# Attention and two expert layers in one kernel: the third tile of scores, the loads of q and k, and the shared tile

## The chip, the core and the metric

The kernel runs on one core of a Trainium2 chip. The time is device microseconds of one execution. The engines are TensorE (PE; its weight loads are listed apart as PEld), VectorE (DVE), ScalarE (ACT), GpSimd (POOL) and SyncE (SP), which here only issues DMAs. A letter q behind an engine's name means its sequencer, which issues DMAs.

## The reference

Three stages follow each other: causal attention of 2 batches x 12 heads, 448 positions, width 64; a layer 768 -> 2048 -> 768 with a leaky activation (slope alpha for each of the 2048); a second one with a piecewise quadratic activation. The 24 heads make 12 pairs.

```
scores = q @ k.T / sqrt(64), masked above the diagonal
attn   = softmax(scores);  x = attn @ v          # 896 tokens x 768
h = x @ w_in;   x = (max(h,0) + alpha*min(h,0)) @ w_out
h = x @ w2_in;  x = where(h>=1, h, where(h<=-1, 0, (h+1)**2/4)) @ w2_out
```

The weights arrive as 64-bit floats and are converted on the chip.

## The kernel before, in words

**Attention** handles one pair of heads at a time. The 448 queries of a head are three tiles of 128 and a rest of 64. Tiles 0, 1, 2 see 128, 256 and 384 keys. The two rests of a pair share one 128-row tile (the shared tile, NQ in the code), whose 448 scores come from one product: the stationary operand `qdiag` (128x128) holds the rest of one head in its upper left quarter and that of the other in its lower right one, with zeros elsewhere.

The loop at the end of the program runs over periods p = 0 to 13, and in period p three pairs are worked on: the scores of pair p (`scores`, L357 on, matmuls L376 and for the shared tile L372), their masking and row minimum on DVE (L383), exponentials on ACT (`expo`, L392), the scaling by the row sums on POOL (`norm`, L399 to L403, with a reciprocal on DVE, L400); for pair p-1 the transposes on PE (`transp`, L430) with copies out of PSUM on ACT and DVE (L439); for pair p-2 the product with v (`attnv`, L446 and L454) and the split of its result x into two parts (`evac_x`, L213 on ACT, L216 on DVE). Every engine works in the order in which the program is written. On PE a period is: scores of tiles 0 and 1, the shared tile, attnv of p-2, transposes of tiles 0 and 1 of p-1, scores of tile 2, transposes of the shared tile and of tile 2 of p-1.

**Banks.** PSUM has 8 banks: s0, s1 (scores, one for each head; tiles 0 and 1 share them, tile 2 takes them again), s2 (shared tile), o (attnv), and two each of t0 and t1 (transposes, L410). A group of matmuls on a bank waits until the readers of its last use are done; for s0 and s1 these are the DVE instructions of L383.

**Loads.** `load` (L330 to L340) brings q and k of one pair (448 KB, L336) and the two quarters of `qdiag` (16 KB each, L340); three buffers each. `load_v` (L342 to L348) brings v in seven pieces. Weights (`Weights.load`, L103) come in chunks of 768 or 512 KB into two buffers. All of them are issued by SP, one after the other, in the order of the program. `prime` converts the first chunks during attention: the magnitude on ACT (L113), then from period 4 on one of five steps per period (four on DVE at L129, L135, L141, L153; the fourth one is L147 on DVE with a cast on ACT, L150).

**The layers** (`run_layer`, matmuls L253) follow with 2304 matmuls of 128x448; a few of them (`early_tiles`) fill the last periods of attention.

Of the kernel before, what the change touches and what calls it, by code (L numbers as in the profile page):

```python
# [8 lines left out]
F32 = mybir.dt.float32  # L9
# [13 lines left out]
def attention_moe_moe_kernel(ctx: ExitStack, tc: tile.TileContext, qk, v, w1, w2, w3, w4, alpha, out):  # L23
# [8 lines left out]
    nc = tc.nc  # L32
    NP, _, _, S = qk.shape
    NB = 2
    CP, D = v.shape[1], v.shape[-1]
# [30 lines left out]
    def warm_up():  # L66

        z = const.tile([128, 512], F32R, tag="zero", name="zero")
        nc.vector.memset(f32(z), 0.0)
        for _ in range(NWARM):  # L70
            ps = ps_o.tile([128, 512], F32, tag="o", name="warm_ps")
            nc.tensor.matmul(ps, lhsT=z[:, :128], rhs=z, start=True, stop=True)

    def constants():
        nc.vector.memset(half, 0.5)
        make_identity(nc, ident)
        for t, p0, n in ((mask, 0, Q), (mask_rest, 0, D), (mask_rest, D, D)):
            if p0 == 0:
                nc.gpsimd.memset(t, 0.0)
            d = t[p0:p0 + n, t.shape[1] - n:]  # L80
            nc.gpsimd.affine_select(
                out=d, in_=d, compare_op=ALU.is_ge, fill=MASK, base=0, pattern=[[-1, n]], channel_multiplier=1
            )


    class Weights:
# [82 lines left out]
        def next(self):  # L169
            self.n_used += 1  # L170
            return self.split.pop(self.n_used - 1)
# [66 lines left out]
    def new_banks():  # L238

        pools = (ps_s, "s0"), (ps_s, "s1"), (ps_s, "s2"), (ps_o, "o"), (ps_t, "t0"), (ps_t, "t1"), (ps_t, "t0"), (ps_t, "t1")  # L240
        while True:
            for pool, tag in pools:
                yield pool.tile([128, 512], F32, tag=tag, name="ps")
# [17 lines left out]
    def early_tiles(batches):  # L261

        for f, bs in enumerate(batches):
            ws = wts.next()
            ps = {b: new_tile() for b in bs}
            early[f] = ws, ps
            for k in range(KD - 1):
                products(ps, ws, x_t, k, k, k == 0, False)
                yield

    def run_layer(layer, late):

        if layer in (1, 3):
            mt, nch, kc, src = NF, 1, KD, x_t
        else:
            mt, nch, kc, src = NM, NC2, KC, g_t
        evac = {1: act_prelu, 2: evac_x, 3: act_quad, 4: evac_out}[layer]
        for m in range(mt):
            ps = {}
            for ch in range(nch):  # L280
                if layer == 1 and m in early:
                    ws, ps = early.pop(m)
                    products(ps, ws, src, kc - 1, kc - 1, False, True)
                else:
                    ws = wts.next()
                rest = {b: new_tile() for b in range(NB) if b not in ps} if ch == 0 else ps

                end = layer == 4 and m == mt - 1 and ch == nch - 1
                for group in [{b: p} for b, p in rest.items()] if end else [rest] if rest else []:
                    for k in range(kc):  # L290
                        kk = ch * kc + k
                        products(group, ws, src, k, kk, kk == 0, kk == nch * kc - 1)
                    if end:
                        interleave(*(evac(p, m, b) for b, p in group.items()), [])
                ps = {**ps, **rest}
                if wts.n_used > 1 and not early:
                    interleave(wts.split_ops(), late)
                    late = []
                    wts.load()
                    wts.magnitude()  # L300
            late = [] if end else [op for pair in zip(*(evac(ps[b], m, b) for b in range(NB))) for op in pair]
        return late


    class Attention:
# [51 lines left out]
        def scores(self, p, tiles):  # L357
            if 0 in tiles:
                self.pexp[p] = self.ap.tile([Q, 2, TRI], F32, tag="pexp", name="pexp", bufs=3)
                self.st[p] = self.ap.tile([Q, 2, 2 * NQ + 1], F32, tag="stat", name="stat", bufs=4)  # L360
            t = self.raw[p]
            if NQ in tiles:
                banks = [self.ps_s.tile([128, 512], F32, tag="s2", name="rest_ps")]
            else:
                banks = [self.ps_s.tile([128, 512], F32, tag=f"s{j}", name=f"s{j}_ps") for j in range(2)]
            off, todo = 0, []
            for i in tiles:
                for n, (e, col) in enumerate(self.rows(p, i)):
                    w = e.shape[1]
                    ps = banks[n][:, off:off + w]  # L370
                    if i == NQ:
                        nc.tensor.matmul(ps, lhsT=self.qdiag[p % 3], rhs=t[:, 1, :], start=True, stop=True)  # L372
                        todo.append((e, ps, mask_rest, col))
                    else:
                        h = slice(n * D, (n + 1) * D)
                        nc.tensor.matmul(  # L376
                            ps, lhsT=t[h, 0, i * Q:(i + 1) * Q], rhs=t[h, 1, :w], start=True, stop=True
                        )
                        todo.append((e, ps, mask[:, REST - w:], col))
                off += w  # L380

            for e, ps, m, col in todo:
                nc.vector.tensor_tensor_reduce(  # L383
                    out=e, in0=ps, in1=m, scale=-SCALE, scalar=3.0e38, op0=ALU.add, op1=ALU.min,
                    accum_out=self.st[p][:, 0, col:col + 1],
                )
# [76 lines left out]
    with tc.manual_schedule():  # L463
        wts = Weights()
        ps_s, ps_t, ps_o = (
            ctx.enter_context(tc.tile_pool(name=f"ps_{n}", bufs=b, space=PSUM))
            for n, b in (("s", 1), ("t", 2), ("o", 1))
        )
        banks = new_banks()
        with ExitStack() as pa:  # L470
            ap = pa.enter_context(tc.tile_pool(name="attn", bufs=2))
            at = Attention(ap, ps_s, ps_t, ps_o)
            at.zeros()
            at.load(0)
            warm_up()
            at.load(1)
            at.load_v(0)
            nc.sync.dma_start(out=alpha_sb, in_=alpha)
            constants()
            early = {}  # L480
            fill = early_tiles(((0, 1), (0,)))
            prime = wts.prime()
            PRIME = 3

            for p in range(NP + 2):
                new, mid, old = p < NP, 1 <= p <= NP, p >= 2  # L490

                def spare():
                    if not new:
                        next(prime, None)
                        next(fill, None)

                if new:
                    at.scores(p, (0, 1))
                    at.scores(p, (NQ,))
                    at.expo(p, (0, 1, NQ))  # L500
                spare()
                if old:
                    at.attnv(p - 2)
                    high, low = at.evac(p - 2)
                    high()
                if p >= PRIME:
                    next(prime, None)
                if mid:
                    at.transp(p - 1, (0, 1))
                if new:  # L510
                    at.scores(p, (2,))
                if old:
                    low()
                if new:
                    at.expo(p, (2,))
                spare()
                if mid:
                    at.transp(p - 1, (NQ,))
                    at.transp(p - 1, (2,))
                if new:  # L520
                    at.norm(p)
                spare()
                if 0 < p < NP - 1:
                    at.load(p + 1)
                if p + 1 < NP:
                    at.load_v(p + 1)
                if p == PRIME - 2:
                    wts.load()
                    wts.load()
            for _ in fill:  # L530
                pass
            for _ in prime:
                pass
        gpool = ctx.enter_context(tc.tile_pool(name="g", bufs=1))
        ep = ctx.enter_context(tc.tile_pool(name="ep", bufs=2))
        late = []
        for layer in (1, 2, 3, 4):
            late = run_layer(layer, late)
            if layer % 2 == 0:
                interleave(late, [])  # L540
                late = []
# [44 lines left out]
```

## Time and profile before

| | |
|---|---|
| median of 3 runs (range) | 563.89 us (562.46 to 571.53) |
| the profiled execution | 563.78 us |
| its span, first to last instruction | 561.9 us |
| PE, PEld busy | 97%, 86% |
| DVE, ACT, POOL busy | 74%, 43%, 24% |
| matmuls of the layers (L253), busy | 234.7 + 233.8 us |
| granted TensorE clock, mean | 0.993 |

The profile is one execution; its span is 1.9 us shorter than its time. The share of a busy engine is a mean over the attention (the first 96 us), where all engines work in turns, and the layers, where PE works nearly alone. Times in the rows are microseconds from the start of the span; idle time in brackets stands before the instruction, with what ended it.

### The profile page before, as it was taken

How to read it: one execution, taken by the hardware profiler on the slowest of the kernel's cores; microseconds unless marked ns; L12 is line 12 of the kernel's file. 1: busy time of each engine (PE TensorE's matmuls, PEld its weight loads, DVE VectorE, ACT ScalarE, POOL GpSimd, SP SyncE). 2: the span in 40 equal slices, each digit the busy share in tenths (PEclk: the TensorE clock that was granted, in tenths of full speed). 3: DMA queues.
4: the chain of work that ended last, by engine and by line, in shares of the span. 5: the costliest groups of instructions: out<-in, count | busy, mean ns of one | idle time of the engine just before them, and what ended most of it. 6: DMA issues, size and time to landing. Idle time of an engine off the chain costs nothing.

```text
span 561.9 us, 8739 instructions
## 1 busy us (share of the span) xinstructions
PE 547.4 (97%) x3195; PEld 482.2 (86%) x3195; DVE 418.4 (74%) x797; ACT 240.6 (43%) x509; POOL 136.6 (24%) x179
## 2 busy tenths in 40 slices
PE   7699999999999999999999999999999999999997
PEld 3456667999999999999999999999999999999996
DVE  4569886888888998765765779888888867555740
ACT  5578984333333333322233345555555433222220
POOL 4526753133333331000000003333333300000000
PEclk9889999999999999999999999999999999999999
DMA  4544511333333223433333523333322244343421
GB/s 122 199 136 117 167 55 58 112 113 113 113 113 113 75 76 113 127 98 113 114 112 88 177 97 108 113 113 113 113 95 75 76 129 143 132 130 128 145 71 33
DMA packets 25674, 62.31 MB, mean 111 GB/s; under 512 B 5280, under 2 KB 13984, under 8 KB 25632
## 3 DMA queue, kind: packets, MB, share of 16 engines
q1 hardware_dynamic: 23760, 60.15, 34.5%
q10 hardware_dynamic: 1872, 1.61, 0.8%
q8 instruction: 25, 0.41, 0.3%
q14 instruction: 17, 0.14, 0.1%
HBM read 58.99 MB, written 2.75 MB: 110 GB/s over the span
## 4 chain that ended last, share of the span: by engine, by line
PE 84%; POOL 0%; DVE 0%; ACT 0%; issue 0%; ACTq 0%
PE ps L253 83%; PE o_ps L446 0%; PE t_ps L430 0%; POOL pexp L403 0%; PE o_ps L454 0%; DVE o_sb L226 0%; ACT o_sb L226 0%; ACTq L226 0%
## 5 line engine op out<-in xcount | busy, mean ns | idle before, releaser
L253 PE MATMUL ps<-x,w_split 128*128 128x448 f32 x1152 | 234.7, 366 | 0.0
L253 PE MATMUL ps<-g,w_split 128*128 128x448 f32 x1152 | 233.8, 365 | 0.0
L253 PEld LDWEIGHTS ps<-g,w_split 128*128 128x128 f32 x1152 | 216.3, 188 | 17.1
L253 PEld LDWEIGHTS ps<-x,w_split 128*128 128x128 f32 x1152 | 216.0, 188 | 17.4
L177 POOL TENSOR_TENSOR g<-act_g,g 128x448 fp32r<-128x448 f32 x64 | 85.5, 1336 | 271.3 <-ACT g L176 271.2
L150 ACT CAST w_split<-w_f 128x512 fp32r<-128x512 f32 (+1 forms) x80 | 56.6, 707 | 125.8 <-DVE w_f L147 86.7
L153 DVE TENSOR_TENSOR w_split<-w_f,w_split 128x512 fp32r<-128x512 f32 (+1 forms) x80 | 66.1, 827 | 52.6 <-ACT w_split L150 52.5
L176 ACT CAST g<-act_g 128x448 fp32r<-128x448 f32 x64 | 36.2, 565 | 76.8 <-DVE act_g L189 62.8
L129 DVE TENSOR_SCALAR w_f<-w_f 128x512 f32<-128x512 f32 (+1 forms) x80 | 58.5, 731 | 9.0 <-ACT w_f L113 8.9
L147 DVE SCALAR_TENSOR_TENSOR w_f<-w_raw,w_f 128x512 uint32<-128x512 uint32 (+1 forms) x80 | 63.6, 795 | 1.4
L141 DVE SCALAR_TENSOR_TENSOR w_f<-w_raw,w_f 128x512 uint32<-128x512 uint32 (+1 forms) x80 | 63.5, 794 | 1.4
L113 ACT ACTIVATE w_f<-w_raw 128x512 f32<-128x512 f32 (+1 forms) x80 | 61.2, 764 | 0.4 <-DMA w_raw<-w 0.4
L392 ACT ACTIVATE pexp<-pexp,stat 128x128 f32<-128x128 f32 (+2 forms) x72 | 35.8, 499 | 16.8 <-DVE stat L383 16.5
L135 DVE TENSOR_SCALAR w_f<-w_f 128x512 uint32<-128x512 uint32 (+1 forms) x80 | 38.2, 478 | 1.4
L201 ACT ACTIVATE act_t<-act_t,half 128x448 f32<-128x448 f32 x32 | 21.5, 672 | 37.7 <-DVE act_t L200 37.7
L403 POOL TENSOR_SCALAR pexp<-pexp,stat 128x128 f32<-128x128 f32 (+2 forms) x72 | 34.5, 494 | 4.7 <-DVE stat L383 3.3
L383 DVE CUSTOM_DVE_ANT_0 pexp<-s_ps,mask 128x128 f32<-128x128 f32 (+2 forms) x72 | 26.2, 413 | 9.6 <-PE s_ps L376 9.2
L376 PE MATMUL s_ps<-qk_raw 64*128 64x128 f32 (+2 forms) x144 | 25.4, 431 | 5.6 <-DMA qk_raw<-qk 4.8
L226 DVE COPY o_sb<-ps 128x224 f32<-128x224 f32 x12 | 4.7, 391 | 29.8 <-ACT o_sb L226 29.8
L439 DVE COPY pt<-t_ps 128x128 f32<-128x128 f32 (+2 forms) x36 | 14.0, 418 | 13.1 <-PE t_ps L430 13.1
L446 PEld LDWEIGHTS o_ps<-pt,v 128*64 128x64 f32 x144 | 9.7, 143 | 14.9 <-ACT pt L439 6.0
L200 DVE TENSOR_SCALAR act_t<-ps 128x448 f32<-128x448 f32 x32 | 19.9, 622 | 3.0 <-PE ps L253 2.4
(47 smaller groups left out, 280.4 us busy)
## 6 DMA issues: line engine op xcount, KB each, us to landing
w_raw<-w SPq DMA_DIRECT2D x32, 768.0 KB, 4.3
w_raw<-w SPq DMA_DIRECT2D x48, 512.0 KB, 3.7
qk_raw<-qk SPq DMA_DIRECT2D x11, 448.0 KB, 3.9
out<-o_sb SPq DMA_DIRECT2D x12, 112.0 KB, 1.7
out<-o_sb ACTq DMA_DIRECT2D x12, 112.0 KB, 1.7
v<-v SPq DMA_DIRECT2D x12, 56.0 KB, 2.7
v<-v SPq DMA_DIRECT2D x12, 48.0 KB, 2.1
v<-v SPq DMA_DIRECT2D x12, 40.0 KB, 2.0
```

Of the source, the lines that this page charges most:

```text
L113: nc.scalar.activation(out=f32(w), in_=f32(hi), func=AF.Abs)
L129: nc.vector.tensor_scalar(out=f32(w), in0=f32(w), scalar1=HI_MIN, scalar2=HI_MAX, op0=ALU.max, op1=ALU.min)
L135: nc.vector.tensor_scalar(out=w, in0=w, scalar1=5, scalar2=2, op0=ALU.logical_shift_left, op1=ALU.logical_shift_right)
L141: nc.vector.scalar_tensor_tensor(out=w, in0=hi, scalar=0xC0000000, in1=w, op0=ALU.bitwise_and, op1=ALU.bitwise_or)
L147: nc.vector.scalar_tensor_tensor(out=w, in0=lo, scalar=29, in1=w, op0=ALU.logical_shift_right, op1=ALU.bitwise_or)
L150: nc.scalar.copy(s[:, 0, :n], f32(w))
L153: nc.vector.tensor_sub(s[:, 1, :n], f32(w), f32(s[:, 0, :n]))
L176: nc.scalar.copy(t[:, 0, :], g)
L177: nc.gpsimd.tensor_sub(t[:, 1, :], g, f32(t[:, 0, :]))
L253: nc.tensor.matmul(ps[b][:, :S], lhsT=ws[:, part, k * 128:(k + 1) * 128], rhs=src[b, kk][:, xp, :], start=first and part == 0 and xp == 0, ...
L392: nc.scalar.activation(out=e, in_=e, func=AF.Exp, bias=st[:, 0, col:col + 1], scale=-1.0, accum_out=st[:, 1, col:col + 1],)
L403: nc.gpsimd.tensor_scalar(out=e, in0=e, scalar1=sums[:, col:col + 1], scalar2=1.0, op0=ALU.mult, op1=ALU.mult)
```

## The change

It has four parts. The third tile of scores of pair 0 goes into the banks t0 and t1 instead of s0 and s1. In period 1 the third tile of scores stands ahead of the transposes of pair 0. The load of q and k of pair p+2 is issued in period p (before: of pair p+1, and none in period 0), and the first two chunks of weights are issued in periods 1 and 2, one in each, behind that load (before: both in period 1). The product of the shared tile is two matmuls, each with 64 columns of `qdiag` and 64 partitions of the result.

```diff
--- before.py
+++ after.py
@@ -362,14 +362,21 @@
             if NQ in tiles:
                 banks = [self.ps_s.tile([128, 512], F32, tag="s2", name="rest_ps")]
             else:
-                banks = [self.ps_s.tile([128, 512], F32, tag=f"s{j}", name=f"s{j}_ps") for j in range(2)]
+
+                pool, tag = (self.ps_t, "t") if p == 0 and 2 in tiles else (self.ps_s, "s")
+                banks = [pool.tile([128, 512], F32, tag=f"{tag}{j}", name=f"{tag}{j}_ps") for j in range(2)]
             off, todo = 0, []
             for i in tiles:
                 for n, (e, col) in enumerate(self.rows(p, i)):
                     w = e.shape[1]
                     ps = banks[n][:, off:off + w]
                     if i == NQ:
-                        nc.tensor.matmul(ps, lhsT=self.qdiag[p % 3], rhs=t[:, 1, :], start=True, stop=True)
+
+                        for j in range(2):
+                            h = slice(j * D, (j + 1) * D)
+                            nc.tensor.matmul(
+                                ps[h], lhsT=self.qdiag[p % 3][:, h], rhs=t[:, 1, :], start=True, stop=True
+                            )
                         todo.append((e, ps, mask_rest, col))
                     else:
                         h = slice(n * D, (n + 1) * D)
@@ -505,9 +512,11 @@
                     high()
                 if p >= PRIME:
                     next(prime, None)
+                if p == 1:
+                    at.scores(p, (2,))
                 if mid:
                     at.transp(p - 1, (0, 1))
-                if new:
+                if new and p != 1:
                     at.scores(p, (2,))
                 if old:
                     low()
@@ -520,12 +529,11 @@
                 if new:
                     at.norm(p)
                 spare()
-                if 0 < p < NP - 1:
-                    at.load(p + 1)
+                if p + 2 < NP:
+                    at.load(p + 2)
                 if p + 1 < NP:
                     at.load_v(p + 1)
-                if p == PRIME - 2:
-                    wts.load()
+                if p in (PRIME - 2, PRIME - 1):
                     wts.load()
             for _ in fill:
                 pass
```

The order of PE's matmuls, from the shared tile of period 0 to the end of period 1, before (s_ps and rest_ps are scores, t_ps is a bank of t0 or t1):

```order
L372 MATMUL rest_ps<-qk_raw,qdiag_83 128x448
L376 MATMUL s_ps<-qk_raw 128x384 x2
L376 MATMUL s_ps<-qk_raw 128x128 x2
L376 MATMUL s_ps<-qk_raw 128x256 x2
L372 MATMUL rest_ps<-qk_raw,qdiag_84 128x448
L430 MATMUL t_ps<-ident,pexp 128x64 x12
L376 MATMUL s_ps<-qk_raw 128x384 x2
L430 MATMUL t_ps<-ident,prest_91 128x64 x8
L430 MATMUL t_ps<-ident,pexp 128x64 x12
```

And the same stretch with the change (L377 and L383 are the matmuls of the scores there, L437 the transposes):

```order
L377 MATMUL rest_ps<-qk_raw,qdiag_83 64x448 x2
L383 MATMUL t_ps<-qk_raw 128x384 x2
L383 MATMUL s_ps<-qk_raw 128x128 x2
L383 MATMUL s_ps<-qk_raw 128x256 x2
L377 MATMUL rest_ps<-qk_raw,qdiag_84 64x448 x2
L383 MATMUL s_ps<-qk_raw 128x384 x2
L437 MATMUL t_ps<-ident,pexp 128x64 x12
L437 MATMUL t_ps<-ident,prest_91 128x64 x8
L437 MATMUL t_ps<-ident,pexp 128x64 x12
```

The 128x384 scores of pair 0 now write a t bank, those of pair 1 stand ahead of twelve transposes, and each shared tile is two products.

SP's DMAs behind the load of alpha, before (v_87, v_88 and v_89 are v of pairs 1, 2 and 3; the first qk_raw here is q and k of pair 2, the second of pair 3; six more pieces of v follow each first one):

```order
L478 DMA alpha_sb<-alpha 128x16
L348 DMA v_87<-v 112x128
...
L336 DMA qk_raw<-qk 128x896
L340 DMA qdiag_85<-qk 64x64 x2
L348 DMA v_88<-v 112x128
...
L103 DMA w_raw<-w 128x1536 x2
L336 DMA qk_raw<-qk 128x896
L340 DMA qdiag_83<-qk 64x64 x2
L348 DMA v_89<-v 112x128
```

With the change (the three qk_raw are pairs 2, 3 and 4):

```order
L485 DMA alpha_sb<-alpha 128x16
L336 DMA qk_raw<-qk 128x896
L340 DMA qdiag_85<-qk 64x64 x2
L348 DMA v_87<-v 112x128
...
L336 DMA qk_raw<-qk 128x896
L340 DMA qdiag_83<-qk 64x64 x2
L348 DMA v_88<-v 112x128
...
L103 DMA w_raw<-w 128x1536
L336 DMA qk_raw<-qk 128x896
L340 DMA qdiag_84<-qk 64x64 x2
```

Each load of q and k has moved ahead of the seven pieces of v that stood before it, and that of pair 3 ahead of both chunks of weights as well.

## Rows read from the trace of the kernel before

**Rows 1.** Chain of waits, its last long piece: start, duration, what.

```profile
96.13 462.29 PE ps L253 x2280
```

**Rows 2.** Busy time by stretch: stretch, length, engines (count), PE clock, DMA share, GB/s.

```profile
21.36:26.11 4.75, 0.00 (x1) 0.03 (x1) 1.82 (x6) 1.88 (x6) 3.08 (x8) 0.90 0.68 251
26.11:35.09 8.98, 8.53 (x75) 4.91 (x76) 3.61 (x17) 4.94 (x16) 0.53 (x1) 0.67 0.46 130
```

**Rows 3.** Timeline of PE, periods 2 to 10: start, duration, instruction, [idle before].

```profile
16.51 1.02 PE L372 MATMUL rest_ps<-qk_raw,qdiag 128*128 128x448 f32 x2
...
26.11 1.65 PE L376 MATMUL s_ps<-qk_raw 64*128 64x128 f32 x8 [4.75 <-DMA qk_raw<-qk]
27.69 1.86 PE L372 MATMUL rest_ps<-qk_raw,qdiag 128*128 128x448 f32 x2
...
35.92 1.02 PE L372 MATMUL rest_ps<-qk_raw,qdiag 128*128 128x448 f32 x2
...
42.05 1.02 PE L372 MATMUL rest_ps<-qk_raw,qdiag 128*128 128x448 f32 x2
...
54.31 1.02 PE L372 MATMUL rest_ps<-qk_raw,qdiag 128*128 128x448 f32 x2
...
60.62 1.02 PE L372 MATMUL rest_ps<-qk_raw,qdiag 128*128 128x448 f32 x2
...
66.75 1.02 PE L372 MATMUL rest_ps<-qk_raw,qdiag 128*128 128x448 f32 x2
...
73.14 1.02 PE L372 MATMUL rest_ps<-qk_raw,qdiag 128*128 128x448 f32 x2
```

**Rows 4.** Timeline of SP's queue: start, time to issue, DMA.

```profile
11.59 0.58 SPq L336 DMA_DIRECT2D qk_raw<-qk  x1
12.29 1.11 SPq L340 DMA_DIRECT2D qdiag<-qk  x2
13.45 3.43 SPq L348 DMA_DIRECT2D v<-v  x7
16.92 1.07 SPq L103 DMA_DIRECT2D w_raw<-w  x2
18.09 0.45 SPq L336 DMA_DIRECT2D qk_raw<-qk  x1
```

**Rows 5.** The tile qk_raw: its loads, from issue to landing.

```profile
DMA to landing us min/median/max: 3.2/3.7/7.9
```

**Rows 6.** Timeline of period 5, PE, its weight loads and DVE.

```profile
42.05 0.30 PEld L372 LDWEIGHTS rest_ps<-qk_raw,qdiag 128*128 128x128 f32 x2 [0.33 <-issue]
...
42.99 0.20 PEld L446 LDWEIGHTS o_ps<-pt,v 128*64 128x64 f32 x4 [0.65 <-ACT pt L439]
43.00 1.52 PE L446 MATMUL o_ps<-pt,v 128*64 128x384 f32 x12
...
43.37 0.14 PEld L446 LDWEIGHTS o_ps<-pt,v 128*64 128x64 f32 x2 [0.18 <-issue]
...
43.69 0.57 PEld L446 LDWEIGHTS o_ps<-pt,v 128*64 128x64 f32 x6 [0.18 <-issue]
...
45.57 0.62 DVE L439 COPY pt<-t_ps 128x128 f32<-128x128 f32 x2 [0.78 <-PE t_ps L430]
...
46.23 0.56 DVE L383 CUSTOM_DVE_ANT_0 pexp<-s_ps,mask 128x384 f32<-128x384 f32 x1
```

**Rows 7.** Timeline of period 7, ACT and PE.

```profile
57.94 0.83 ACT L150 CAST w_split<-w_f 128x768 fp32r<-128x768 f32 x1
...
59.30 0.68 PE L430 MATMUL t_ps<-ident,pexp 64*128 64x64 f32 x12 [0.60 <-POOL pexp L403]
```

**Rows 8.** Timeline, end of period 1: POOL, DVE, weight loads.

```profile
13.69 1.15 POOL L403 TENSOR_SCALAR pexp<-pexp,stat 128x384 f32<-128x384 f32 x2
...
14.29 0.56 DVE L383 CUSTOM_DVE_ANT_0 pexp<-s_ps,mask 128x384 f32<-128x384 f32 x1
...
15.63 0.55 PEld L376 LDWEIGHTS s_ps<-qk_raw 64*128 64x128 f32 x8 [0.34 <-DVE stat L383]
```

## The prediction

> **What bounds the kernel.** First the chain of waits: its last piece runs from 96.13 us to the end, 462.29 us of layer matmuls on PE [rows 1]. The change touches none of them, so it can only move the moment at which that stretch begins. All that follows is about the first 96 us.
>
> Second the busy time by stretch [rows 2]. From 21.36 to 26.11 PE does nothing, and in the 8.98 us behind that its granted clock is 0.67 on average: it ran partly at 1.2 GHz, partly at 2.4. The clock began to fall within the idle stretch (0.90 there). Third the timeline of PE [rows 3], where I measure each period from one shared tile to the next: 11.18 us (16.51 to 27.69, with an idle stretch of 4.75 that ends with the load of q and k), 8.23 (to 35.92, the slow clock), 6.13 (to 42.05), 12.26 for two (to 54.31), 6.31, 6.13 and 6.39 (to 73.14). So an ordinary period is 6.13 us, and two early ones are far above it. Fourth SP's queue [rows 4]: the load of pair 3 is issued at 18.09, behind two chunks of weights at 16.92. Loads of q and k land 3.7 us after issue in the median and 7.9 at most [rows 5]; 18.09 + 7.9 = 25.99, just when PE goes on at 26.11. The weights ahead of it held this load up.
>
> What makes 6.13 is read from one period [rows 6]. DVE sits idle 0.78 us until the transposes, copies them out (45.57), then reduces the third tile of scores (46.23); these reductions give the banks s0 and s1 back, and only then PE can write the next pair's scores, its shared tile, attnv and the transposes. PE's stretch from scores to transposes lies on this loop; DVE's weight steps lie in its idle 0.78.
>
> **The change part by part.** The sum is made against the profiled execution, 563.78 us, whose span is 561.9; the median is 563.89, 0.1 higher.
>
> *Start.* SP takes 3.43 us to issue v of one pair [rows 4]. Without v ahead of it, the load of pair 2 goes at 11.59 - 3.43 = 8.2 us in place of 11.59, so it lands at 11.9 and not at 15.3 (median 3.7), just before the scores of pair 2 begin (15.63 [rows 8]). In period 1 the third tile's reduction began at 14.29 because the transposes, which wait for POOL, stood ahead of it; now it follows its scores directly, about 1.3 us earlier, and s0 and s1 are free in time. What is late next is POOL: it finishes scaling pair 0 at 13.69 + 1.15 = 14.84 [rows 8], and the last twelve transposes need about 0.4 us behind that. So the scores of pair 2 can begin at about 15.2, 0.4 us earlier. The third tile of pair 0 in the t banks gives nothing by itself that I can find (PE was busy with the shared tile until then, and DVE's next work waits for the row sums); the halves in period 0 may add 0.1. I take 0.5; the ends are 0 (POOL later by as much) and 0.9.
>
> *Halves of the shared tile.* Rows of before have no such product, but attnv has its shape: 64 columns in each half, adjacent matmuls on both halves. Its second and third weight loads begin 0.32 us apart (43.37, 43.69) for 384 columns, so a pass streams 384 columns in 0.32 us, both halves side by side: all twelve matmuls take 1.52 us, while their 3072 columns one after another would take 2.56 [rows 6]. A pass of 448 columns is then 0.373, two are 0.75. The shared tile now takes 42.99 - 42.05 = 0.94 until attnv's first load; the other 0.2 us are its first load and the emptying of the array before the mode changes. With halves the first load is about 0.06 (attnv's first pass: 42.99 to 43.37 = 0.38, less 0.32), attnv keeps the mode, and its first load goes under the running pass. That is 0.75 + 0.06 and no 0.06 later: 0.2 us less per pair. The ends are 0.25 less (the 0.33 idle ahead of it shrinks too) and 1.1 more (everything in series, the rival below). I take the attnv rows, the nearest.
>
> It counts where PE sets the period. In period 7 ACT does: it runs a cast of 0.83 us ahead of the copies that free a t bank, and PE waits 0.60 for its last transposes [rows 7]; period 9, with the magnitude of a chunk there, takes 6.39. I count nothing in these two.
>
> *Loads of pairs 3 to 5.* One pair costs SP 0.58 + 1.11 + 3.43 and small gaps, 5.3 us: pair 3 is issued at 8.2 + 5.3 = 13.5 and lands at 17.2 (21.4 at the maximum). With the shared tile of pair 2 at 16.0 and a period of 5.93, that of pair 3 starts at 21.95, its scores 0.9 earlier at 21.1. The wait of 4.75 goes. Pair 4 goes behind one chunk, at 19.5: it lands between 23.2 and 27.4, and is needed at 27.4. Pair 5, behind the other chunk, at 25.4: between 29.1 and 33.3, needed at 33.3. v is issued later by one load, and needed two periods after it: covered. The chunks, later by 2 and 8 us, are needed in periods 3 and 9: covered. If this cover of a few us for pairs 4 and 5 is gone, each us late is a us of PE.
>
> *Clock.* Without the idle stretch period 3 runs at 2.4 GHz. It has the magnitude on ACT as period 9 has, so I give it 6.39: the shared tile of pair 4 starts at 28.34.
>
> **The sum.** Pair 2 0.5 us earlier; pair 3 27.69 - 21.95 = 5.74; pair 4 35.92 - 28.34 = 7.58; then 0.2 in periods 4, 5, 6, 8, 10 and 11, 1.2 in all: 8.78. The layers start 8.8 us earlier, at 87.3: 563.78 - 8.78 = **555.0 us**, 1.6% less. With start and halves at their unfavourable small ends (0) it is 556.9; with all at the favourable ones, period 3 at 5.93 and the halves in periods 7 and 9 too, 553.3.
>
> **Rivals.** *Loads still late.* Pairs 4 and 5 have no slack at the maximum of 7.9, and SP may issue v slower behind weights. For it: weights straight ahead of q and k made the 7.9. Against: that was behind two chunks, now one. 1 to 2 us: 556 to 557. Chance 0.10.
>
> *The clock falls in period 1.* With pair 0's third tile elsewhere PE finishes pair 1's early scores sooner and then waits for DVE, some 2 us. The one drop seen came with 4.75 us of idle PE. Price as in period 3, 8.23 - 6.39 = 1.84: 556.8. Chance 0.07.
>
> *Weight loads lie bare.* Each shared tile has four loads instead of two, all on the same rows; bare, at 0.14 each, they make it 0.75 + 0.56 = 1.31, 0.37 more than now. In the eight periods that count this is 3.0 and takes 1.4 of gains away: 559.4. Against it stand attnv's rows: twelve loads of 0.14 bare would be 1.7 us on top of 1.28 us of streaming, and the whole takes 1.52 [rows 6]. Chance 0.05. The Trainium skill, "TensorE: Matmul & The Clock Gate", Part 3 on row/col tiling, states this as a rule: weight loads overlap running matmuls only when the row group differs. By that rule the change would give this rival's time; the trace of attnv disagrees with it.
>
> *Slower: the halves in series.* If the two halves run one after the other with their loads bare, a shared tile is 4 x 0.373 + 4 x 0.14 = 2.05, 1.1 more than now, in eleven periods 12.1, against 7.3 won elsewhere: 568.6. It decides from 0.66 us per pair on. Against it again attnv's 1.52. Chance 0.04.
>
> *The order of loads was not the cause*: pair 3 stays late, only start and halves count, 562. Chance 0.02, since issue and landing fit so well. Better than 553.3, by a loop shortened beyond what I see: 0.02. The forecast keeps 0.70.
>
> **The numbers.** The range 553.0 to 558.0 takes in the forecast's own ends, the late loads and the clock; it leaves out bare loads, series, no effect and better, 0.13, and some of the edges. 2% is 11.3 us, about what a measurement of this kernel can tell from no change: faster than 552.6 needs nearly all favourable ends and more, 0.05; slower than 575 needs a series dearer than I priced, 0.01; within 2%, 0.94.
>
> **What would show it.** SP issues pair 3's load near 13.5, ahead of any weights. PE has no idle stretch above 2 us behind its first scores, and the granted clock is 1.00 from 8 us on. Shared tiles start near 16.0, 22.0 and 28.3, then 5.9 apart; from the first load of a shared tile to attnv's first it takes 0.8. The layers' long piece starts near 87.3 and still takes 462.3. I am wrong if PE waits for qk_raw again, if the shared tile takes 1.3 or more, or if periods stay at 6.1 although it takes 0.8, since then another loop (POOL's scaling, ACT) carries them.

## The result, and the profile after

The changed kernel takes **555.99 us** (median of 4 runs, 555.47 to 557.51), the kernel before 563.19 beside it (562.46 to 571.53): ratio 0.9881, 95% interval 0.9858 to 0.9904, 7.2 us less. The prediction was 555.0 within 553.0 to 558.0. Some executions of the kernel before and of the experiments took 8 us or more longer than the rest (571.53 here; in the two of them that were profiled, both_weights and no_order_late, the layers' long piece took 471.40 us instead of 462.29), and they are left out of every ratio, so a median or a range that still holds one stands high.

The profiled execution of the changed kernel is its slowest, 557.51 us with a span of 555.7, and the mean granted clock was 0.994. The three others went with their mean clock: 556.49 (0.996), 555.48 (0.999), 555.47 (1.000).

The chain of waits, last long piece (start, duration), answers to [rows 1]: the layers start 6.23 us earlier and take as long as before.

```profile
89.90 462.29 PE ps L253 x2280
```

The timeline of PE (start, duration, instruction, [idle before]), from the first shared tile (L377; scores L383, transposes L437, attnv L453), answers to [rows 3] and to PE's row of [rows 7]:

```profile
5.87 1.52 PE L377 MATMUL rest_ps<-qk_raw,qdiag 128*64 128x448 f32 x4
...
11.65 0.93 PE L383 MATMUL s_ps<-qk_raw 64*128 64x384 f32 x3 [1.85 <-DVE stat L390]
...
14.10 1.09 PE L437 MATMUL t_ps<-ident,pexp 64*128 64x64 f32 x12 [0.36 <-POOL pexp L410]
14.98 1.59 PE L383 MATMUL s_ps<-qk_raw 64*128 64x128 f32 x8
16.51 1.76 PE L377 MATMUL rest_ps<-qk_raw,qdiag 128*64 128x448 f32 x4
18.05 2.77 PE L453 MATMUL o_ps<-pt,v 128*64 128x384 f32 x12
...
24.49 0.97 PE L377 MATMUL rest_ps<-qk_raw,qdiag 128*64 128x448 f32 x4
...
30.87 0.97 PE L377 MATMUL rest_ps<-qk_raw,qdiag 128*64 128x448 f32 x4
...
36.80 0.97 PE L377 MATMUL rest_ps<-qk_raw,qdiag 128*64 128x448 f32 x4
...
48.72 0.97 PE L377 MATMUL rest_ps<-qk_raw,qdiag 128*64 128x448 f32 x4
...
53.66 0.68 PE L437 MATMUL t_ps<-ident,pexp 64*128 64x64 f32 x12 [0.74 <-POOL pexp L410]
...
54.98 0.97 PE L377 MATMUL rest_ps<-qk_raw,qdiag 128*64 128x448 f32 x4
...
67.30 0.97 PE L377 MATMUL rest_ps<-qk_raw,qdiag 128*64 128x448 f32 x4
...
73.23 0.97 PE L377 MATMUL rest_ps<-qk_raw,qdiag 128*64 128x448 f32 x4
```

The wait of 4.75 us for q and k is gone. Read the periods from shared tile to shared tile: 7.98 (from 16.51), 6.38, 5.93, 11.92 for two, 6.26 (period 7, with the wait for the last transposes), 12.32 for two, 5.93. All but the first are within 0.06 of the forecast's. The first is 2.05 too long, and pair 2's shared tile starts where it did before. There the matmuls are slow: attnv takes 2.77 us instead of 1.5. The busy time by stretch says why (stretch, length, engines PE, PEld, DVE, ACT, POOL, then PE clock, DMA share, GB/s):

```profile
8.00:12.00 4.00, 2.15 (x16) 0.92 (x13) 2.59 (x16) 3.14 (x13) 1.28 (x4) 1.00 0.56 149
12.00:16.00 4.00, 3.63 (x44) 3.04 (x42) 3.06 (x11) 3.84 (x14) 2.59 (x6) 0.73 0.49 123
16.00:20.00 4.00, 4.00 (x16) 1.47 (x14) 1.83 (x10) 2.63 (x10) 3.37 (x7) 0.50 0.33 95
20.00:24.00 4.00, 4.00 (x65) 3.15 (x62) 2.08 (x7) 1.90 (x6) 0.00 (x0) 0.92 0.80 264
```

The granted clock (1 is 2.4 GHz) fell behind the idle stretch of 1.85 us that ends at 11.65: from 16 to 20 us it is 0.50, that is 1.2 GHz. This is the rival "the clock falls in period 1", in the execution that was profiled.

SP's queue answers to [rows 4], and the landing times to [rows 5]:

```profile
8.27 0.43 SPq L336 DMA_DIRECT2D qk_raw<-qk  x1
...
13.50 0.53 SPq L336 DMA_DIRECT2D qk_raw<-qk  x1
...
19.73 0.58 SPq L103 DMA_DIRECT2D w_raw<-w  x1
20.42 0.38 SPq L336 DMA_DIRECT2D qk_raw<-qk  x1
...
26.51 0.58 SPq L103 DMA_DIRECT2D w_raw<-w  x1
27.20 0.38 SPq L336 DMA_DIRECT2D qk_raw<-qk  x1
```

```profile
DMA to landing us min/median/max: 2.9/3.6/5.4
```

Pair 3 goes at 13.50, ahead of any weights, as forecast, and lands in 3.5 us instead of 7.9. Pairs 4 and 5 go at 20.42 and 27.20, not at the forecast's 19.5 and 25.4: SP took 4.46 and 4.48 us over the seven pieces of v ahead of them, not 3.43. Pair 5, straight behind a chunk, took 5.1 us and was in time.

Period 5 on PE, its weight loads and DVE answers to [rows 6]:

```profile
36.80 0.20 PEld L377 LDWEIGHTS rest_ps<-qk_raw,qdiag 128*64 128x64 f32 x4 [0.33 <-issue]
36.80 0.97 PE L377 MATMUL rest_ps<-qk_raw,qdiag 128*64 128x448 f32 x4
...
37.44 0.30 PEld L453 LDWEIGHTS o_ps<-pt,v 128*64 128x64 f32 x4 [0.45 <-ACT pt L446]
...
37.60 1.47 PE L453 MATMUL o_ps<-pt,v 128*64 128x384 f32 x12
...
40.12 0.62 DVE L446 COPY pt<-t_ps 128x128 f32<-128x128 f32 x2 [0.57 <-PE t_ps L437]
```

From the shared tile to attnv's first matmul it is 37.60 - 36.80 = 0.80, as forecast. Before it was 0.95 between the two matmuls (43.00 - 42.05), and attnv itself took 1.52 instead of 1.47: together the 0.2 of the period. By the profile attnv's first load (37.44) begins before the shared tile's last pass has ended (37.77), and DVE's idle time ahead of its copies has shrunk from 0.78 to 0.57.

### The profile page after: what moved, and what is told of

Same layout as the page of the kernel before. It is cut to its first block, busy times and chain, and to the rows that moved or that the text cites. A ratio compares the mean times of both kernels' runs of the same rounds, so it can differ in the third digit from the quotient of the medians.

```text
span 555.7 us, 8784 instructions
## 1 busy us (share of the span) xinstructions
PE 544.4 (98%) x3219; PEld 482.0 (87%) x3219; DVE 418.4 (75%) x797; ACT 239.8 (43%) x509; POOL 136.7 (25%) x179
## 4 chain that ended last, share of the span: by engine, by line
PE 84%; POOL 0%; DVE 0%; ACT 0%; issue 0%; ACTq 0%
PE ps L253 84%; PE o_ps L453 0%; PE t_ps L437 0%; POOL pexp L410 0%; PE o_ps L461 0%; DVE o_sb L226 0%; ACT o_sb L226 0%; ACTq L226 0%
## 5 line engine op out<-in xcount | busy, mean ns | idle before, releaser
L383 PE MATMUL s_ps<-qk_raw 64*128 64x128 f32 (+2 forms) x140 | 23.9, 423 | 1.8 <-DVE stat L390 1.8
L453 PEld LDWEIGHTS o_ps<-pt,v 128*64 128x64 f32 x144 | 10.7, 144 | 12.8 <-issue 6.7
```

## The experiments

The theory was that the loads give the larger part, the halves 1.2 us, and that order and banks in period 1 give nothing or are cancelled by the slow clock. The kernel before ran beside each group on the same chip: 563.29 us (experiments 1 to 3), 563.14 (4, 5 and both_weights), 562.99 (the others of 6) and 563.18 (7).

**1. The order of loads alone** (loads_only: the kernel before with this edit).

```diff
-                if 0 < p < NP - 1:
-                    at.load(p + 1)
+                if p + 2 < NP:
+                    at.load(p + 2)
...
-                if p == PRIME - 2:
-                    wts.load()
+                if p in (PRIME - 2, PRIME - 1):
                     wts.load()
```

> The kernel before with the new order of loads alone (q and k two pairs ahead, one chunk of weights in each of periods 1 and 2); whole shared tile, old order in periods 0 and 1. Theory 1 (the idle 4.75 us and the slow clock behind it were the load's lateness, and little else goes): the shared tile of pair 3 at about 22.6 us, of pair 4 at 29.0, periods of 6.13 behind them, 6.5 to 7 us below the kernel before, 556.5. Rival (the gain is the halves and the order too, the loads alone only trade the wait for another): 559 or more, with an idle stretch of PE above 1 us in period 3.

556.55 us against 563.29; ratio 0.9884 (0.9869 to 0.9899). Its shared tiles on PE:

```profile
16.66 1.02 PE L372 MATMUL rest_ps<-qk_raw,qdiag 128*128 128x448 f32 x2
...
22.79 1.02 PE L372 MATMUL rest_ps<-qk_raw,qdiag 128*128 128x448 f32 x2
...
29.18 1.02 PE L372 MATMUL rest_ps<-qk_raw,qdiag 128*128 128x448 f32 x2
```

Both long periods of before are gone (6.13 and 6.39, no wait, no slow clock): 6.7 us, nearly the whole gain.

**2. The halves alone** (halves_only: the kernel before with the change of the shared tile's product, the piece of the diff with `for j in range(2):` and `ps[h]`).

> The kernel before with the two half products of the shared tile alone. Theory 1 (0.2 us less per pair wherever PE sets the period): periods of 5.93 in place of 6.13, 1.2 to 1.6 us below the kernel before, about 561.8; the wait for q and k of pair 3 stays. Rival (POOL's and ACT's chains carry the period): periods stay at 6.1, within 0.3 us of the kernel before.

562.05 us; ratio 0.9979 (0.9969 to 0.9989), 1.2 us. The wait for q and k stands as it was:

```profile
26.14 1.65 PE L381 MATMUL s_ps<-qk_raw 64*128 64x128 f32 x8 [4.92 <-DMA qk_raw<-qk]
27.72 1.76 PE L375 MATMUL rest_ps<-qk_raw,qdiag 128*64 128x448 f32 x4
```

From pair 3's shared tile to the layers it is 94.97 - 27.72 = 67.25, before 96.13 - 27.69 = 68.44: 1.19 us, the forecast's 1.2.

**3. Without banks and order in period 1** (no_order: the changed kernel with two pieces of the diff undone, that of `pool, tag` and that of `p == 1`), and the changed kernel once more on the same chip (after_again).

> The changed kernel with the third tile of pair 0 back in s0 and s1 and the old order in period 1; loads and halves stay. Theory 1 (the order brings 0.4 us at the start and nothing else): 0.4 us above the changed kernel, 555.9. Rival (the new order leaves PE idle 1.85 us in period 1, the granted clock falls there in many executions, and that costs more than it gains): granted clock 1.00 from 8 us on, the scores of pair 2 start near 15.6 and run at the full clock, 555.0 or less, and the runs lie closer together than the changed kernel's 555.5 to 557.5.

> The changed kernel once more, for its spread and a second profile. If the clock falls in period 1 only in some executions: times from 555.4 to 557.6 that go with the mean granted clock, high clock with low time. If not: all within 0.3 us of each other.

556.38 (555.28 to 556.86) and 556.11 (555.26 to 557.51); ratios 0.9880 (0.9864 to 0.9895) and 0.9880 (0.9862 to 0.9898). Of the changed kernel's four executions three went with the mean clock here (555.26 at 1.000, 556.06 and 556.17 at 0.996), but the slowest, 557.51, has 1.000 as well. Neither theory's clean case came: in the profile without banks and order the start was slow for another reason.

```profile
11.92 1.76 PE L375 MATMUL rest_ps<-qk_raw,qdiag 128*64 128x448 f32 x4
...
17.89 0.97 PE L375 MATMUL rest_ps<-qk_raw,qdiag 128*64 128x448 f32 x4
```

The shared tile of period 1 still takes 1.76 us, its duration in the changed kernel at a granted clock of 0.50, though this trace's clock column says 1.00 there and no idle stretch above 0.7 us went before. So PE began slow in every profile, and when it became fast differed; the clock column does not show it. The 557.51 at a mean clock of 1.000 may be such a late start, but it was not profiled. The medians say that banks and order together give nothing that can be measured here: each interval reaches some 0.9 us to either side, so the 0.4 of the theory would not be seen.

**4. The old order in period 1, the banks kept** (no_p1).

```diff
-                if p == 1:
-                    at.scores(p, (2,))
                 if mid:
                     at.transp(p - 1, (0, 1))
-                if new and p != 1:
+                if new:
```

> The changed kernel with the old order in period 1 (transposes ahead of the third tile); the third tile of pair 0 stays in the t banks. Theory 1 (the t banks give nothing by themselves): DVE's reduction of pair 1's third tile back behind the copies, at 13.9 or later, shared tile of pair 2 not before 16.3 at the full clock. Rival (the t banks are the useful half of the new order): shared tile of pair 2 at 16.0. The clock may fall here too, since PE waits for POOL in period 1: 555.7 to 557.5.

556.18 (555.64 to 556.66); ratio 0.9875 (0.9858 to 0.9891). PE waits in the same place, now for POOL in front of the transposes:

```profile
11.33 0.62 PE L437 MATMUL t_ps<-ident,pexp 64*128 64x64 f32 x4 [1.60 <-POOL pexp L410]
...
14.94 1.59 PE L383 MATMUL s_ps<-qk_raw 64*128 64x128 f32 x8
16.46 1.29 PE L377 MATMUL rest_ps<-qk_raw,qdiag 128*64 128x448 f32 x4
```

The scores of pair 2 start at 14.94, with the new order at 14.98, and both at the slow clock. The order gains these scores nothing: what is waited for is seen on DVE and POOL of the changed kernel (timeline of period 1).

```profile
8.27 0.56 DVE L390 CUSTOM_DVE_ANT_0 pexp<-t_ps,mask 128x384 f32<-128x384 f32 x1
...
10.39 0.25 POOL L406 TENSOR_SCALAR stat<-stat 128x7 f32<-128x7 f32 x1 [6.17 <-ACT pexp L399]
...
10.67 0.20 DVE L407 RECIPROCAL stat<-stat 128x7 f32<-128x7 f32 x1 [1.35 <-POOL stat L406]
...
12.59 0.56 DVE L390 CUSTOM_DVE_ANT_0 pexp<-s_ps,mask 128x384 f32<-128x384 f32 x1
```

DVE's reciprocal for pair 0 stands ahead of the reductions of pair 1 and waits for POOL, and POOL for pair 0's last exponentials on ACT. PE's 1.85 us is this wait. The third tile of pair 1 is reduced at 12.59 instead of 14.29 [rows 8], but pair 2's scores stand behind the transposes that POOL releases: POOL's row sums at 10.39 plus 4.5 us (to the first weight load of the scores). In the kernel before it was 10.89 plus 4.7, with loads_only 11.31 plus 4.3. The place follows POOL.

**5. Four products of zeros on PE in period 1** (warm4: bank o, no result used; `keep_warm` issues that many), then the same **with the zeros written first on DVE** (warm4_early).

```diff
                 if p == 1:
+                    keep_warm(zero, 4)
                     at.scores(p, (2,))
```

> The changed kernel with four matmuls of zeros (128x512, into the bank o, which nobody reads until period 2) in period 1 ahead of the third tile of scores, where PE sat idle 1.85 us. Theory (that idle stretch lets the granted clock fall from about 13 to 17 or 20 us, in some executions longer than in others, and this is the spread): granted clock 1.00 from 8 us on, shared tile of pair 2 near 16.0 and of pair 3 near 22.0, layers from about 87.4, every run between 555.0 and 555.6. Rival (zeros or these few matmuls do not hold the clock, or the spread has another cause): spread and median as in the changed kernel, 555.3 to 557.5, 556.1.

> As the kernel with four matmuls of zeros in period 1, and the zeros for the first three warming matmuls are written as DVE's first work, so that these begin about 0.5 us earlier. Theory: the clock rises earlier than 7.1 to 7.4 us, by up to 0.5, and since the shared tile of pair 0 runs at the slow clock until then, 0.1 to 0.4 us less: 554.8 to 555.3. Rival (the moment of the rise does not follow the start of the matmuls): no difference to the kernel without it beyond 0.1.

warm4: 556.21 (556.1 to 564.69), ratio 0.9893 (0.986 to 0.9926). Of the five executions in that ratio four lie within 0.14 us, all at a mean clock of 1.000; the fifth took 560.20 at 0.997. In the profile the clock is 1.00 in every stretch of attention, so there the zeros held it. That the spread of the changed kernel is that of the clock alone is not shown, since 560.20 came with the zeros too. No execution reached the 555.0 to 555.6 of the theory: four products were too many, pair 1's third tile came only at 13.04. warm4_early: the three executions in the ratio, 0.989 (0.9868 to 0.9912), took 556.37 to 558.02; the three left out took 564.86, 565.52 and 1080.43. The 554.8 to 555.3 of the theory did not come, and whether the moment when PE becomes fast follows its first matmul cannot be told. The profile shows the forecast's start, and then another wait:

```profile
15.76 0.97 PE L376 MATMUL rest_ps<-qk_raw,qdiag 128*64 128x448 f32 x4
...
21.70 0.97 PE L376 MATMUL rest_ps<-qk_raw,qdiag 128*64 128x448 f32 x4
...
34.82 1.60 PE L382 MATMUL s_ps<-qk_raw 64*128 64x128 f32 x8 [1.93 <-DMA qk_raw<-qk]
```

Pair 5's load, straight behind the second chunk, landed 6.5 us after its issue (5.1 in the changed kernel), and PE, earlier now, waited 1.93: the rival "loads still late".

**6. Where the second chunk of weights goes**: with the first in period 1 (both_weights); in period 6 (late_chunk); in period 6 without banks and order (no_order_late); in period 6 with three products of zeros, written early (warm3_early_late).

```diff
-                if p in (PRIME - 2, PRIME - 1):
+                if p in (PRIME - 2, PRIME + 3):
                     wts.load()
```

In both_weights both calls stand in period PRIME - 2 = 1, as in the kernel before.

> The changed kernel with both first chunks of weights in period 1, behind the load of pair 3. Theory 1 (what stands between weights and a load of q and k decides): pair 4's load, issued near 20 behind two chunks, lands after 27 (7 to 8 us) and PE waits for it 0.5 to 1.5 us in period 4: 556.6 to 557.5. Rival (one load ahead is enough and the second chunk's place does not matter): no wait for qk_raw, 556.1.

> The changed kernel with only the second chunk of weights moved from period 2 to period 6. Theory (without a wait for pair 5's load the chunk's place is worth nothing): the same as the changed kernel, 556.0 within 0.4; the load of pair 5 lands in under 4.5 us after its issue. Rival (the chunk costs something in some executions): 555.5 or less. Another rival (the chunk is needed early): 557 or more.

> The changed kernel with the third tile of pair 0 in the score banks and period 1 in the order of before, and the second chunk issued in period 6: only halves and loads are left. Theory (order and banks in period 1 give nothing, POOL's scaling of pair 0 sets the scores of pair 2): shared tile of pair 2 near 16.4, pair 3 near 22.3, layers near 88, 556.0, the same as the changed kernel within 0.4. Rival (order and banks are worth the 0.5 of the prediction): 556.5 or more.

> The changed kernel with three products of zeros on PE in period 1 (the zeros written first on DVE) and the second chunk of weights issued in period 6, not 2. Theory (the start's gain was cancelled by the idle stretch of 1.85 us and the slow clock behind it; in the kernel with zeros pair 5's load was late only because a chunk went ahead of it): shared tiles of pairs 2 to 5 start near 15.8, 21.7, 28.1 and 34.0, no wait for qk_raw on PE, the load of pair 5 lands under 4.5 us after issue, the layers' long piece starts near 87.2, and the time is about 555.0. Rival (loads are late whatever goes ahead of them, or the zeros cost what they keep): a wait for qk_raw of 1 us or more, or shared tiles later than 16.5, and 556 or more.

both_weights: 555.53 and 556.04 in the two executions in the ratio, 0.9868 (0.9845 to 0.9891), and 564.60 to 566.80 in the four left out; pair 4's load took 6.8 us behind both chunks and still PE did not wait for it (it landed at 27.4, the scores began at 28.0), so the theory's wait missed. late_chunk: 556.67 (555.45 to 557.47), ratio 0.988 (0.9865 to 0.9895): not told apart from the changed kernel, though the median lies outside the 0.4 of the theory; pair 5's load lands in 3.5 us, but nobody had waited. no_order_late: 556.82 (555.62 to 564.73), ratio 0.9889 (0.987 to 0.9909), shared tiles at 16.62 and 22.55, layers at 88.01: near the places expected, the time not told apart.

The profiles of no_order_late (old banks and order) and both_weights (new ones) have pair 2 at a granted clock of 1.00, and POOL's row sums of pair 0 at almost the same moment:

```profile
11.27 0.25 POOL L404 TENSOR_SCALAR stat<-stat 128x7 f32<-128x7 f32 x1 [7.06 <-ACT pexp L397]
...
16.62 0.97 PE L375 MATMUL rest_ps<-qk_raw,qdiag 128*64 128x448 f32 x4
```

```profile
11.34 0.25 POOL L406 TENSOR_SCALAR stat<-stat 128x7 f32<-128x7 f32 x1 [7.11 <-ACT pexp L399]
...
16.52 0.97 PE L377 MATMUL rest_ps<-qk_raw,qdiag 128*64 128x448 f32 x4
```

Pair 2's scores begin 4.38 us behind the row sums in both (15.65 and 15.72). Its shared tile begins 5.35 behind them with the old order and 5.18 with the new one: order and banks together are worth 0.17 us there. What the banks give alone was not run at the full clock.

warm3_early_late: 555.33 (555.21 to 557.91), ratio 0.9876 (0.9859 to 0.9893). Its profile, the slowest of its five executions, has pairs 2 to 5 at the places expected (15.88, 21.82, 28.20, 34.14) and no wait up to pair 8, then the chunk is in the way again:

```profile
59.30 1.65 PE L382 MATMUL s_ps<-qk_raw 64*128 64x128 f32 x8 [1.83 <-DMA qk_raw<-qk]
60.88 1.76 PE L376 MATMUL rest_ps<-qk_raw,qdiag 128*64 128x448 f32 x4
```

Pair 9's load went straight behind the chunk in period 6 and took 6.3 us. A chunk straight ahead of a load costs it some 1.4 to 2.9 us in whichever period (5.0 to 6.5 in all profiles, where the median of the other loads is 3.6), and once PE has idled for it the clock falls too (1.76 for a shared tile). The theory was right on pair 5 and had not asked who stands behind the chunk in its new place.

**7. The chunk behind the load of pair 5 and ahead of v** (warm3_behind), with the three products of zeros.

```diff
                     at.load(p + 2)
+                if p == PRIME:
+                    wts.load()
                 if p + 1 < NP:
                     at.load_v(p + 1)
-                if p in (PRIME - 2, PRIME - 1):
+                if p == PRIME - 2:
                     wts.load()
```

> The changed kernel with the three products of zeros in period 1 (zeros written first on DVE) as before, and the second chunk of weights in period 3, issued behind the load of pair 5 and ahead of that period's v. Theory (a chunk straight ahead of a load of q and k makes it land 6.3 to 6.8 us after issue, and behind it the load lands as if alone): pair 5's load lands under 4.5 us after issue, pair 6's too since v's issue lies between, no wait for qk_raw on PE in any period up to 6, shared tiles near 15.9, 21.8, 28.2, 34.1, 40.1, the long piece of the layers starts near 87.5, and 555.2. Rival (the wait moves once more, to v of pair 4, behind the chunk now, or to pair 6): a wait of 1 us or more for v or qk_raw, and 556 or more.

**555.30 us** (554.92 to 555.89), ratio 0.9864 (0.9848 to 0.9881), 0.7 to 0.8 below the two medians of the changed kernel, whose intervals overlap with it. PE and the chain:

```profile
10.30 1.62 PE L71 MATMUL warm_ps<-zero 128*128 128x512 f32 x3
12.19 0.93 PE L382 MATMUL s_ps<-qk_raw 64*128 64x384 f32 x3 [0.27 <-DVE stat L389]
...
16.11 0.97 PE L376 MATMUL rest_ps<-qk_raw,qdiag 128*64 128x448 f32 x4
...
22.04 0.97 PE L376 MATMUL rest_ps<-qk_raw,qdiag 128*64 128x448 f32 x4
...
28.42 0.97 PE L376 MATMUL rest_ps<-qk_raw,qdiag 128*64 128x448 f32 x4
```

```profile
87.59 462.29 PE ps L252 x2280
```

No wait for q and k behind the first pair, the clock at 1.00 in every stretch of attention, pair 5's load in 4.0 us and pair 6's in 3.4: this is the course that the prediction had drawn (16.0, 21.95, 28.34, layers at 87.3).

## Why the prediction was right, and where it was not

**Loads: right.** Pair 3's load, issued 4.6 us earlier and landing 4.4 sooner after its issue, took away the wait and the slow clock behind it. Alone the loads give 6.7 us; the sum's terms for them, without the start, were (27.69 - 16.51 - 6.13) + (35.92 - 27.69 - 6.39) = 6.9.

**Halves: right.** 0.80 from shared tile to attnv, 5.93 a period, none in period 7, where PE waits 0.74 for its last transposes, and 6.38 in period 9, 1.19 us in all. The rivals with bare loads or halves in series are refuted by the same 0.80 (they had 1.31 and 2.05). The rule of the Trainium skill ("TensorE: Matmul & The Clock Gate", Part 3 on row/col tiling), that weight loads overlap running matmuls only when the row group differs, does not hold here by this trace: all four loads of the shared tile use all rows, as do those of attnv behind them, and attnv's first one begins under the shared tile's last pass.

**Start: the step that failed.** The prediction gave 0.5 us to the earlier reduction in period 1 and to a load that lands in time. The reduction did come 1.7 earlier, and it bought pair 2's scores nothing: with either order they stand 4.38 behind POOL's row sums of pair 0 at the full clock, and only the shared tile behind them gains 0.17 (experiment 6). The prediction had seen that POOL is late next, but not that the old order stands behind POOL by just as much. In the kernel before the scores began 0.79 behind POOL's last scaling (14.84 to 15.63) instead of some 0.4; that was most likely the load of pair 2, which landed 3.9 behind its issue at 11.59, at 15.5, so the load was, most likely, the useful half of this term. POOL's moment is set by pair 0's last exponentials. It moved by 0.5 in the profiled execution (10.89 to 10.39), and so did pair 2's scores, but by then the clock had fallen and the shared tile came at 16.51 all the same, 6.12 behind the row sums instead of 5.18. POOL's moment follows when PE becomes fast at the start, which differs between executions of one kernel: 10.39 and 10.55 in the changed kernel's two profiles, where pair 0's shared tile takes 1.52 and 1.70 us, and 11.34 in both_weights, where the third tile behind it is slow too (1.65 instead of 0.92). With the old banks and order and a third tile nearly as slow (1.59) it is 11.27, so no part of order and banks shows in it.

**Clock: the size that was off.** The forecast said 1.00 from 8 us on, and gave the fall in period 1 a chance of 0.07. Of the five profiles with the t banks and without zeros (the changed kernel twice, no_p1, late_chunk, both_weights) four showed it or part of it. The idle time was right (forecast some 2 us, measured 1.85), its chance was not, and its price varies: the period behind is 7.98 - 5.93 = 2.05 too long in the changed kernel's first profile and as much in late_chunk, but 0.44 in its second and 0.32 in no_p1, for a forecast of 1.84. To this comes the 6.12 - 5.18 = 0.94 that the slow clock had cost pair 2's shared tile before that, which the rival left out: without the fall it would have come at 10.39 + 5.18 = 15.57, an estimate from both_weights. Against the forecast pair 2 is late by 16.51 - 16.0 = 0.5, and 0.5 + 2.05 = 2.55 is the whole distance in the profiled execution: layers at 89.90 instead of 87.3.

**Loads still late: did not come in the profiles of the changed kernel, with little to spare.** There a load straight behind one chunk took 5.1 to 5.4 us and nobody waited: pair 5's landed at 27.20 + 5.1 = 32.3, and PE, late from the start, needed it only at about 35.5. In warm3_behind, where the start was on time, pair 5's scores begin at 33.03, so 32.3 would do there, with 0.7 to spare; in warm4_early the load took 6.5 and PE waited 1.93.

So the median is 1.0 above the forecast, and the fastest (555.26) is within 0.3 of it. The profiles put the difference on the clock that falls in a part of the executions; for the executions without a profile, and for the 557.51 at a mean clock of 1.000 above all, this is argued and not shown. Open is what decides, in one execution and not in the next, when PE becomes fast at the start, whether the clock falls for the length of the idle stretch or for that moment (the two went together: the one profile that kept the clock became fast latest and idled least), and whether the 0.8 us between the sum of experiments 1 and 2 (6.74 + 1.24) and the change's 7.2 is all of this: the intervals overlap.

## What to carry to other kernels

Look at what stands straight ahead of a load in its queue, and who waits for that load: here its place gave 6.7 of 7.2 us, and every place for the chunk of weights straight ahead of a load delayed that load; with the pieces of v in between the next load landed in 3.4 us. When an instruction is moved forward, follow the engine behind it to what it waits for next; the third tile came 1.7 us earlier and gained 0.17. And an idle stretch of under 2 us on TensorE may cost as much again in slow clock, or more (0.94 + 2.05 us behind 1.85): price it as likely.

## What was not expected of the hardware

- The clock fell behind idle stretches of 1.85, 1.84 (twice) and 1.60 us in period 1, and not behind one of 1.42 (both_weights, shared tile at 16.52 in 0.97 us). It fell too behind the waits of 1.93 us in period 5 of warm4_early and of 1.83 us in period 9 of warm3_early_late.
- PE begins slow, by durations (1.76 for a shared tile that takes 0.97 later), until some 7 to 10 us in most profiles and about 17 in one (no_order); the granted clock in the record is 1.00 there.
- Over all profiles a load of 448 KB straight behind one chunk of 768 KB took 5.0 to 6.5 us from issue to landing (35 loads), and behind two 6.8 to 7.9 (3 loads). The 116 others took 3.6 in the median, but four of them 4.8 to 6.5 (the longest pair 7's in late_chunk) with no chunk straight ahead; why is open.
